# One input row loaded as 16 short rows and spread on the chip, with the query weights moved ahead in ScalarE's queue of loads

## The chip, the cores and the metric

The kernel runs on one NeuronCore of one Trainium2 chip. The metric is the device time of one launch in microseconds (us). Three runs of the kernel before gave a median of 193.31 us (193.21 to 193.57). One further execution was recorded by the hardware profiler. All durations and waits below come from that execution.

The core has five engines with a queue of instructions each: TensorE (PE; its loads of weights are shown as PEld), VectorE (DVE), ScalarE (ACT), GpSimd (POOL) and SyncE (SP). In this kernel SP and ACT also issue the DMAs, which 16 DMA engines carry out. The profile calls the DMA queue that SP fills q1 and the one that ACT fills q10.

## The reference

One token is decoded. With x of 512 values, the reference computes (cut to what matters):

```
xn = layernorm(x)
q  = xn @ wq                       # 32 heads of 128
s  = softmax(q k^T / sqrt(128)) v  # per head, the last 4096 of 32768 cached keys
s  = s @ wo                        # 4096 -> 512
x1 = xn + hs                       # hs = 0 here: a shift along a sequence of length 1
g  = silu(x1 + gelu(layernorm(x1) @ w3) @ w4)
out = x + s * g
```

All inputs are bfloat16. Keys and values of the window are 32 x 4096 x 128 values each, 33.6 MB each. The weights wq and wo have 4.2 MB each; w2, w3 and w4 have 3.3 MB together.

## The kernel before, in words

**Tiling.** The 32 heads are worked in 8 groups of G = 4. A group's keys are one tile `kv` of 128 partitions x 32768 bytes, 4.2 MB, and so are its values. The partitions hold 32 stretches of keys of each of 4 heads. K tiles come from a pool of three buffers, V tiles from a pool of two. The V pool (line 539) is opened in the place of the pool `wts`, which holds the weights wq, w2, w3, w4 and some small tiles of the head of the kernel, once these are done with.

**Scores.** Of each K tile, 64 or 80 of the 128 columns of keys go to VectorE, in four parts: `k_vector` multiplies by the query, spread over the partitions in `q_bc` (line 321), and adds up (line 323). The others are turned by TensorE (line 339), copied out by ScalarE (line 342) and multiplied by `q_pair` (line 350). Softmax and the values follow two steps behind (LAG = 2): `sm_exp` on ScalarE, `v_wide` on TensorE (line 427).

**Order.** The loop over steps (from line 533) is written out by hand for PE, DVE and ACT. Ahead of it, in the head of the kernel, a scheduler orders the instructions of each engine. SP's loads go through `load` (lines 75 and 76), which keeps them in the order of the program: w2, w3, w4 (two pieces), K of group 0 in two halves, K of group 1, K of group 2, V of group 0, K of group 3, and so on. A load into a buffer waits until its former reader is done. Eight completion semaphores of DMAs are given out in turn over SP's and ACT's loads together; a load that gets one which was used before waits for the landing of that earlier load first.

**The head.** ACT issues three loads (lines 79, 82 and 84):

- `x_bf`: x as 128 partitions of 4 values (128 rows of 8 bytes), for the layernorm;
- `x_row`: x as 4 rows of 128 values on partitions 0, 32, 64 and 96, after GpSimd has cleared the tile. `xn_row` (line 242) and the last addition (line 656) read it;
- `wq_sb`: the query weights, 128 rows of 32768 bytes.

Then line 183 turns `x_bf` into float32 `x_f`. `ln_stats` (lines 158 to 179) adds it up by TensorE and takes mean and variance. Lines 186 to 196 give `xq_bf`, the normed x in the order that wq wants. Lines 203 to 209 multiply it by wq (32 products, `qr_ps`). Lines 210 to 218 copy and spread the result into `q_bc`, and lines 219 to 226 make `q_pair`. Between them stand the multi-layer part (lines 228 to 280: a second layernorm, `a_ps` by line 252 with a gelu in line 255, w4 in line 270, `g_row` in line 280) and `make_masks` (lines 126 to 141), which makes small tables of ones and zeros from the identity for the end of the kernel.

**Places in memory.** The pools stand one behind the other in each partition: K, kt, prod, const, small, sm, and then wts (later the V pool). The first tile in `small` is an unused one of 192 bytes (line 71, `pad`). With it the K tiles start at bytes 16512, 49280 and 82048 of each partition, `wq_sb` at 151808, and the V tiles at 160000 and 192768.

**The end.** The last group's V comes in three pieces (64, 32 and 32 columns), and two loads of rows of wo follow it. After the last piece has landed come 32 products (line 461), a multiplication (line 471), 16 products with the rows of wo (line 155), lines 654 and 656, and the store.

Of the kernel before, what the change touches and what calls it, by code (L numbers as in the profile page):

```python
# [8 lines left out]
P = 128  # L9
BF16 = mybir.dt.bfloat16  # L10
FP32 = mybir.dt.float32
ACT = mybir.ActivationFunctionType
ALU = mybir.AluOpType
AX = mybir.AxisListType
# [12 lines left out]
def kernel(  # L27
# [14 lines left out]
    nc = tc.nc  # L42

    Bb, Sq, D = A_x.shape
    assert Bb == 1 and Sq == 1, "decode kernel: B == Sq == 1"
    _, H, Sk, Dh = A_k_cache.shape
    HD = A_wq.shape[1]
# [6 lines left out]
    KC = D // P  # L54
# [9 lines left out]
    small = ctx.enter_context(tc.tile_pool(name="small", bufs=1))  # L64
    ps_misc = ctx.enter_context(tc.tile_pool(name="ps_misc", bufs=1, space=PSUM))
# [7 lines left out]
    wts = wts_guard.__enter__()  # L73

    def load(dst, src):
        return tc.keep_in_program_order(nc.sync.dma_start(out=dst, in_=src))  # L76

    x_bf = small.tile([P, KC], BF16, name="x_bf")
    nc.scalar.dma_start(out=x_bf[:], in_=A_x.rearrange("a b (p c) -> p (a b c)", p=P))
    x_row = small.tile([P, P], BF16, name="x_row")  # L80
    nc.gpsimd.memset(x_row[:], 0.0)
    nc.scalar.dma_start(out=x_row[0:P:32, :], in_=A_x.rearrange("a b (j n) -> (a b j) n", j=KC))
    wq_sb = wts.tile([P, KC, HD], BF16, name="wq_sb")
    nc.scalar.dma_start(out=wq_sb[:].rearrange("p c n -> p (c n)"),
                        in_=A_wq.rearrange("(a b c) n -> b a (c n)", a=4, c=KC))
    w2_sb = wts.tile([P, KC, D], BF16, name="w2_sb")
    load(w2_sb[:], B_w2.rearrange("(p c) n -> p c n", p=P))
    w3_sb = wts.tile([P, KC, F], BF16, name="w3_sb")
# [14 lines left out]
    ident_bf = const.tile([P, P], BF16, name="ident_bf")  # L103
# [54 lines left out]
    def ln_stats(src_f, tag):  # L158
        ps = ps_misc.tile([P, KC], FP32, tag="misc", name="ln_ps")
        nc.tensor.matmul(ps[:], lhsT=ones_f[:], rhs=src_f, start=True, stop=True)  # L160
        tot = small.tile([P, 1], FP32, name=f"ln_tot_{tag}")
        nc.vector.reduce_sum(out=tot[:], in_=ps[:], axis=AX.X)
        negmean = small.tile([P, 1], FP32, name=f"ln_negmean_{tag}")
        nc.vector.tensor_scalar(out=negmean[:], in0=tot[:], scalar1=-1.0 / D,
                                scalar2=None, op0=ALU.mult)
        xc = small.tile([P, KC], FP32, name=f"ln_xc_{tag}")
        nc.vector.tensor_scalar(out=xc[:], in0=src_f, scalar1=negmean[:], scalar2=None,
                                op0=ALU.add)
        sq = small.tile([P, KC], FP32, name=f"ln_sq_{tag}")
        nc.vector.tensor_tensor(out=sq[:], in0=xc[:], in1=xc[:], op=ALU.mult)  # L170
        ps2 = ps_misc.tile([P, KC], FP32, tag="misc", name="ln_ps2")
        nc.tensor.matmul(ps2[:], lhsT=ones_f[:], rhs=sq[:], start=True, stop=True)
        vtot = small.tile([P, 1], FP32, name=f"ln_vtot_{tag}")
        nc.vector.reduce_sum(out=vtot[:], in_=ps2[:], axis=AX.X)
        rstd = small.tile([P, 1], FP32, name=f"ln_rstd_{tag}")
        nc.vector.tensor_scalar(out=rstd[:], in0=vtot[:], scalar1=1.0 / D,
                                scalar2=LN_EPS, op0=ALU.mult, op1=ALU.add)
        nc.gpsimd.tensor_tensor(out=rstd[:], in0=rstd[:], in1=neg_half[:, 0:1], op=ALU.pow)
        return xc, negmean, rstd


    x_f = small.tile([P, KC], FP32, name="x_f")
    nc.vector.tensor_copy(out=x_f[:], in_=x_bf[:])
    xc, negmean, rstd = ln_stats(x_f[:], "x")
    xn_f = small.tile([P, KC], FP32, name="xn_f")
    nc.vector.tensor_scalar(out=xn_f[:], in0=xc[:], scalar1=rstd[:], scalar2=None, op0=ALU.mult)
# [16 lines left out]
    for b in range(2):  # L203
        zeros(qr[b][:])
        for c in range(KC):
            wc = wq_sb[:, c, :].rearrange("p (g a d) -> p g a d", a=G, d=Dh)
            for a in range(G):
                nc.tensor.matmul(qr[b][32 * a:32 * a + 1], lhsT=xq_bf[:, c:c + 1], rhs=wc[:, 4 * b:4 * b + 4, a, :],  # L208
                                 start=False, stop=(c == KC - 1), skip_group_check=True)
    nc.scalar.copy(out=q_row[:, 0:4, 0, :], in_=qr[0][:])  # L210
    nc.vector.tensor_copy(out=q_row[:, 4:8, 0, :], in_=qr[1][:])  # L211
    for b in range(2):
        qb_ps = ps_tr.tile([P, 4, Dh], FP32, tag="pt", name="qb_ps")
        nc.tensor.matmul(qb_ps[:], lhsT=sel[:].rearrange("k b a -> k (b a)"), rhs=q_row[:, 4 * b:4 * b + 4, 0, :],
                         start=True, stop=True)
        nc.scalar.copy(out=q_bc[:, 4 * b:4 * b + 4, :], in_=qb_ps[:])
    for b in range(2):
# [5 lines left out]
        for t in range(2):  # L223
            rows = slice(64 * t, 64 * t + 64)
            nc.scalar.copy(out=q_pair[rows, 4 * b:4 * b + 4, :, G * t:G * t + G].rearrange("p g l a -> p g a l"),  # L225
                           in_=qt_ps[rows].bitcast(BF16).rearrange("p g (a m l) -> p g a m l", a=G, l=2)[:, :, :, 0, :])
# [4 lines left out]
    for j in range(KC):  # L231
        for c in range(KC):
            nc.tensor.matmul(hs_ps[:, j:j + 1], lhsT=w2_sb[:, c, j::4],
                             rhs=shifted_bf[:, c:c + 1], start=(c == 0), stop=(c == KC - 1))
# [30 lines left out]
    for i in range(11):  # L265
        n = P if i < 10 else 96
        terms.append((a_bf[0:n, i % 3, i // 3:i // 3 + 1], w4_sb[0:n, i, :]))
    for i, (col, w) in enumerate(terms):
        r = 32 * (i % 4)
        nc.tensor.matmul(hr_ps[r:r + 1].rearrange("r j n -> r (j n)"), lhsT=col, rhs=w, start=False,  # L270
                         stop=(i >= len(terms) - 4), skip_group_check=True)
# [25 lines left out]
                            op=ALU.max)  # L297
    par_t = const.tile([1 + G, PB, G], FP32, name="par_t")
    nc.vector.tensor_scalar(out=par_t[:],
                            in0=ident_f[0:1 + G, 1:1 + G].unsqueeze(1).to_broadcast([1 + G, PB, G]),  # L300
# [387 lines left out]
```

## Time and profile before

| what | us |
|---|---|
| median of 3 runs (range) | 193.31 (193.21 to 193.57) |
| the profiled execution, its own time | 193.37 |
| its span, first to last instruction | 191.2 |
| outside the span (193.37 - 191.2) | 2.2 |
| busy: DVE, PE, ACT, POOL | 150.9, 121.2, 89.5, 2.4 |
| share of q1 and q10 of the 16 DMA engines' span | 91.6%, 5.1% |
| bytes moved | 79.02 MB |

How to read it: the busy time of an engine is a sum over the whole span, and a high sum alone does not make it the bound. The span is also shown cut in 40 slices of 4.78 us, with a digit for the busy tenths of each engine and of the DMA engines. The windows view gives the same for any stretch of time, with the rate of the DMA engines. The chain of waits follows the end of the kernel back to what released each step. "Landing" is when the last of the DMA engines that took part reports that its share of a transfer is done. The trace also holds a record of every DMA packet: queue, start, duration and size. Here a packet is one row of a transfer.

### The profile page before, as it was taken

Reading aid. Unit: us, or ns where it says so; the run is one execution under the profiler, and the core shown is the slowest. Engines: PE = TensorE matmul, PEld = TensorE weight load, DVE = VectorE, ACT = ScalarE, POOL = GpSimd, SP = SyncE. Lnnn points to the kernel's source line nnn. Section 1 sums busy time; section 2 is a strip of 40 time slices with the busy share of each in tenths; the row PEclk is TensorE's granted clock in tenths of the full one; section 3 lists DMA queues with packets and bytes.
Section 4 is the critical chain, followed back from the end, with each engine's and each line's share of the span. In section 5 each row is a group of like instructions: output and inputs, shape, how many; then the busy total and the mean of one; then the engine's idle time right before and its main releaser. Section 6 shows DMA issues by size and latency. Waiting matters only on the chain.

```text
span 191.2 us, 2843 instructions
## 1 busy us (share of the span) xinstructions
PE 121.2 (63%) x1161; PEld 77.0 (40%) x1161; DVE 150.9 (79%) x175; ACT 89.5 (47%) x191; POOL 2.4 (1%) x11
## 2 busy tenths in 40 slices
PE   1554853989826368356945773681889289749772
PEld 0430222767615334243434432540764078513321
DVE  1560169979999999999999999999999997990111
ACT  2001270887795076527364654552575147743120
POOL 2110000000000000000000000000000000000000
PEclk9999696555665556955585579558555855996999
DMA  6999999999999999999999999999999998999990
GB/s 202 436 444 410 431 425 432 439 439 437 432 440 432 432 428 439 439 439 418 428 418 425 439 428 408 456 432 435 439 439 434 428 432 379 471 435 394 415 372 29
DMA packets 4572, 79.02 MB, mean 413 GB/s; under 512 B 624, under 2 KB 1232, under 8 KB 1488
## 3 DMA queue, kind: packets, MB, share of 16 engines
q1 hardware_dynamic: 4264, 74.65, 91.6%
q10 hardware_dynamic: 296, 4.20, 5.1%
q8 instruction: 9, 0.15, 0.3%
q14 instruction: 3, 0.02, 0.0%
HBM read 78.84 MB, written 0.00 MB: 412 GB/s over the span
## 4 chain that ended last, share of the span: by engine, by line
DVE 47%; DMA 42%; PE 6%; ACT 1%; issue 1%; SPq 1%; DVEq 0%; ACTq 0%
DMA kv<-in_A_k_cache_dram 31%; DVE S L323 28%; DVE prod L321 16%; DMA kv<-in_A_v_cache_dram 9%; PE pt L339 3%; DMA x_bf<-in_A_x_dram 2%; ACT kt L342 1%; PE ov L427 1%; PE sT L350 1%; DVE m L366 1%; SPq L76 1%; DVE S L364 1%; DVE mx L374 1%; PE oT L461 1%; PE ot_ps L444 0%
## 5 line engine op out<-in xcount | busy, mean ns | idle before, releaser
L323 DVE TENSOR_REDUCE S<-prod 128x20 f32<-128x2560 bf16 (+1 forms) x32 | 86.0, 2686 | 1.1
L342 ACT COPY kt<-pt 128x1024 bf16<-128x1024 bf16 x52 | 51.4, 1013 | 40.0 <-PE pt L339 38.1
L339 PE MATMUL pt<-ident_f,kv 128*128 128x128 f32 x208 | 49.2, 392 | 10.0 <-DMA kv<-in_A_k_cache_dram 10.0
L321 DVE TENSOR_TENSOR prod<-kv,q_bc 128x2560 bf16<-128x2560 bf16 (+1 forms) x32 | 45.4, 1417 | 3.6 <-ACT q_pair L225 1.8
L339 PEld LDWEIGHTS pt<-ident_f,kv 128*128 128x128 f32 x208 | 36.2, 205 | 13.9 <-DMA kv<-in_A_k_cache_dram 9.3
L350 PE MATMUL sT<-q_pair,kt 128*128 128x8 bf16 x416 | 19.6, 170 | 14.9 <-ACT kt L342 14.8
L350 PEld LDWEIGHTS <-kt 128*128 128x128 bf16 x416 | 16.9, 105 | 26.1 <-ACT kt L342 24.9
L427 PE MATMUL ov<-kv,pT 128*16 128x512 bf16 x248 | 23.2, 536 | 1.2 <-DMA kv<-in_A_v_cache_dram 1.2
L388 ACT ACTIVATE pT<-S,mb 128x128 bf16<-128x128 f32 x32 | 13.9, 572 | 0.3
L372 PE MATMUL mt_ps<-ident_f,m 128*1 128x128 f32 x8 | 2.9, 360 | 16.6 <-DVE rden L399 16.1
L433 ACT COPY ov_sb<-ov 128x512 f32<-128x512 f32 x8 | 4.7, 586 | 18.4 <-PE ov L427 18.4
L427 PEld LDWEIGHTS <-pT 128*16 128x16 bf16 x248 | 6.9, 112 | 14.3 <-issue 12.7
L359 ACT ACTIVATE own<-sT,par 128x48 f32<-128x48 f32 (+1 forms) x32 | 7.5, 356 | 3.7 <-PE sT L350 3.7
L444 PE MATMUL ot_ps<-ident_f,ov_sb 128*128 128x128 f32 x32 | 7.5, 379 | 2.2 <-ACT mb L384 1.7
L211 DVE CAST q_row<-qr_ps 128x512 bf16<-128x512 f32 x1 | 0.7, 692 | 10.0 <-PE qr_ps L208 10.0
L388 ACT ACTIVATION_READ_ACCUMULATOR pT<-S,mb 128x1 f32 x32 | 8.3, 258 | 0.0
L372 PEld LDWEIGHTS mt_ps<-ident_f,m 128*1 128x1 f32 x8 | 0.6, 80 | 17.1 <-DVE rden L399 16.4
L399 DVE RECIPROCAL rden<-den_ps 128x4 f32<-128x4 f32 x8 | 1.4, 175 | 6.7 <-PE den_ps L394 6.7
L381 PE MATMUL mb_ps<-md,par_t 5*128 5x4 f32 x16 | 3.9, 311 | 4.1 <-DVE md L376 4.1
L255 ACT ACTIVATE a_row<-a_ps 128x384 bf16<-128x384 f32 x1 | 0.5, 491 | 12.1 <-remote 12.1
L444 PEld LDWEIGHTS ot_ps<-ident_f,ov_sb 128*128 128x128 f32 x32 | 4.8, 188 | 3.2 <-ACT mb L384 2.1
L208 PE MATMUL qr_ps<-wq_sb,xq_bf 128*1 128x512 bf16 x32 | 3.5, 611 | 3.6 <-DMA wq_sb<-in_A_wq_dram 3.6
(122 smaller groups left out, 82.8 us busy)
## 6 DMA issues: line engine op xcount, KB each, us to landing
kv<-in_A_k_cache_dram SPq DMA_DIRECT2D x7, 4096.0 KB, 31.0
kv<-in_A_v_cache_dram SPq DMA_DIRECT2D x7, 4096.0 KB, 30.6
wq_sb<-in_A_wq_dram ACTq DMA_DIRECT2D x1, 4096.0 KB, 17.5
kv<-in_A_k_cache_dram SPq DMA_DIRECT2D x2, 2048.0 KB, 27.5
wo<-in_A_wo_dram SPq DMA_DIRECT2D x1, 2048.0 KB
kv<-in_A_v_cache_dram SPq DMA_DIRECT2D x1, 2048.0 KB
kv<-in_A_v_cache_dram SPq DMA_DIRECT2D x2, 1024.0 KB, 16.3
w_sb<-in_B_w_dram SPq DMA_DIRECT2D x1, 1376.0 KB, 10.3
```

The source lines that it names most:

```text
L208: nc.tensor.matmul(qr[b][32 * a:32 * a + 1], lhsT=xq_bf[:, c:c + 1], rhs=wc[:, 4 * b:4 * b + 4, a, :], start=False, stop=(c == KC - 1), sk ...
L321: nc.vector.tensor_tensor(out=prod[:, 0:m, :], in0=kn[:, rows, :], in1=q_bc[:, g:g + 1, :].to_broadcast([P, m, Dh]), op=ALU.mult)
L323: nc.vector.tensor_reduce(out=st[g]["S"][:, rows], in_=prod[:, 0:m, :], axis=AX.X, op=ALU.add)
L339: nc.tensor.transpose(pt[:, i, :], kn[:, c:c + 2, :].rearrange("p c d -> p (c d)").bitcast(FP32), ident_f[:])
L342: nc.scalar.copy(out=kts[b][:, 0:n, :], in_=pt[:, 0:n, :].bitcast(BF16))
L350: nc.tensor.matmul(st[g]["sT"][:, c:c + 2, :].rearrange("p c a -> p (c a)"), lhsT=kt[:, i, l::2], rhs=q_pair[:, g, l, :], start=(l == 0), ...
L359: nc.scalar.mul(s["own"][:, 0:m, a], s["sT"][:, 0:m, a], par[:, a:a + 1])
L381: nc.tensor.matmul(mb_ps[:], lhsT=par_t[:].rearrange("k b a -> k (b a)"), rhs=md[:], start=True, stop=True)
L388: nc.scalar.activation(out=s["pT"][:, :, a], in_=s["S"][:], func=ACT.Exp, scale=scale, bias=mb[:, a:a + 1], accum_out=s["sum"][:, a:a + 1])
L427: nc.tensor.matmul(ov[r:r + 4 * G], lhsT=s["pT"][:, c:c + 4, :].rearrange("p i a -> p (i a)"), rhs=v[:, c:c + 4, :], start=(i < 4), stop=( ...
L433: nc.scalar.copy(out=s["ov_sb"][:], in_=ov[:])
L444: nc.tensor.transpose(ot_ps[:, step * j:step * j + P], s["ov_sb"][:, j, :], ident_f[:])
```

## The change

```diff
-    x_bf = small.tile([P, KC], BF16, name="x_bf")
-    nc.scalar.dma_start(out=x_bf[:], in_=A_x.rearrange("a b (p c) -> p (a b c)", p=P))
+    XR, XC = 16, D // 16
+    x_in = small.tile([XR, XC], BF16, name="x_in")
+    nc.scalar.dma_start(out=x_in[:], in_=A_x.rearrange("a b (r n) -> (a b r) n", r=XR))
+    wq_sb = wts.tile([P, KC, HD], BF16, name="wq_sb")
+    nc.scalar.dma_start(out=wq_sb[:].rearrange("p c n -> p (c n)"),
+                        in_=A_wq.rearrange("(a b c) n -> b a (c n)", a=4, c=KC))
     x_row = small.tile([P, P], BF16, name="x_row")
     nc.gpsimd.memset(x_row[:], 0.0)
     nc.scalar.dma_start(out=x_row[0:P:32, :], in_=A_x.rearrange("a b (j n) -> (a b j) n", j=KC))
-    wq_sb = wts.tile([P, KC, HD], BF16, name="wq_sb")
-    nc.scalar.dma_start(out=wq_sb[:].rearrange("p c n -> p (c n)"),
-                        in_=A_wq.rearrange("(a b c) n -> b a (c n)", a=4, c=KC))
...
+    m8 = P // XR
+    x_up = wts.tile([XR, XR, m8], BF16, name="x_up")
+    nc.vector.tensor_copy(out=x_up[:], in_=ident_bf[0:XR, 0:XR].unsqueeze(2).to_broadcast([XR, XR, m8]))
+    x_own = wts.tile([P, m8], BF16, name="x_own")
+    nc.vector.tensor_reduce(out=x_own[:], in_=ident_bf[:].rearrange("d (i t) -> d t i", t=m8), axis=AX.X, op=ALU.max)
+    x_all = ps_misc.tile([P, m8, KC], FP32, tag="misc", name="x_all")
+    nc.tensor.matmul(x_all[:].rearrange("p t c -> p (t c)"), lhsT=x_up[:].rearrange("k r t -> k (r t)"), rhs=x_in[:],
+                     start=True, stop=True)
+    x_pick = wts.tile([P, m8, KC], FP32, name="x_pick")
+    nc.vector.tensor_tensor(out=x_pick[:], in0=x_all[:], in1=x_own[:].unsqueeze(2).to_broadcast([P, m8, KC]), op=ALU.mult)
     x_f = small.tile([P, KC], FP32, name="x_f")
-    nc.vector.tensor_copy(out=x_f[:], in_=x_bf[:])
+    nc.vector.tensor_reduce(out=x_f[:], in_=x_pick[:].rearrange("p t c -> p c t"), axis=AX.X, op=ALU.add)
```

x for the layernorm comes as 16 rows of 32 values. One product with `x_up` (ones where column d belongs to row d/8) repeats each row on 8 partitions, the table `x_own` keeps on each partition the four values that are its own, and a sum over the 8 places gives `x_f` as before. The load of wq is ACT's second, that of `x_row` its third.

What the built program shows of the change, beyond the diff:

- The tile `x_in` takes 64 bytes of each partition where `x_bf` took 32 (8, rounded up). All later tiles of `small`, `sm`, `wts` and the V pool start 32 bytes further on: `wq_sb` at 151840, V at 160032 and 192800. K stays where it was.
- The load of K of group 2 waits for the landing of wq, where it waited for `x_row`: it has been given the same completion semaphore.
- On DVE, most of `make_masks` stands between the steps of the first layernorm, where before it stood between those of the second; `xn_row` stands directly ahead of the copy `q_row` (before: ahead of `xq_bf`).
- On PE, the last of the 20 products of `a_ps` stands behind the 32 with wq. On ACT, a load of an activation table and the gelu of `a_row` follow the first copy into `q_row`, where before they stood ahead of it; there is one load of a table more.

## The prediction

> **What bounds the kernel now.** I read the windows view first, for the rate of the DMA engines:
>
> ```profile
> core 0: us, PE busy (x) PEld busy (x) DVE busy (x) ACT busy (x) POOL busy (x), PEclk, DMA share, GB/s
> 0.00:4.78 4.78, 0.61 (x1) 0.10 (x1) 0.52 (x6) 1.28 (x1) 1.24 (x9) 1.00 0.67 202
> 4.78:184.00 179.22, 117.17 (x1096) 75.15 (x1098) 149.43 (x165) 87.57 (x189) 1.11 (x2) 0.69 1.00 430
> 184.00:191.20 7.20, 3.43 (x70) 1.75 (x62) 0.98 (x4) 0.60 (x2) 0.00 (x0) 0.97 0.34 128
> ```
>
> From 4.78 to 184 us the 16 DMA engines are busy all the time (share 1.00) at 430 GB/s. The packet records agree: the first packet starts at 1.78 us, the last large one ends at 187.2 us, and a 32768-byte row takes 1213 ns (median) whatever it belongs to. 79.02 MB at 430 GB/s are 183.8 us; with 1.78 us ahead, some slow first packets, and what follows the last byte (187.2 to 191.2), that is the span. So the stream of bytes is the bound, if it never runs dry. The longest pieces of the chain of waits tell about that:
>
> ```profile
> 0.74 4.03 DMA x_bf<-in_A_x_dram
> 5.36 36.62 DMA kv<-in_A_k_cache_dram
> ...
> 130.42 23.05 DMA kv<-in_A_k_cache_dram
> 168.94 17.25 DMA kv<-in_A_v_cache_dram
> ```
>
> The chain puts x_bf at its head, since SP's fourth load of K waited for the semaphore of x_bf. It is not a cause: the K tile issued at 5.36 us landed 36.6 us later, and the records show its first row starting at 29.9 us. It stood in the queue for over 24 us. The load of the last group's V, issued from 168.9 us on, needs 17.25 us, of which its own 4.19 MB are 9.8 us at 430 GB/s: some 7 us of other work still stood ahead. At 130.4 us the same sum gives 13 us. So a delay of compute by less than about 7 us leaves the engines fed.
>
> Next, what waits in the head:
>
> ```profile
> 4.79 0.17 DVE L183 CAST x_f<-x_bf 128x4 f32<-128x4 bf16 x1 [3.45 <-DMA x_bf<-in_A_x_dram]
> ...
> 19.87 3.45 PE L208 MATMUL qr_ps<-wq_sb,xq_bf 128*1 128x512 bf16 x32 [3.61 <-DMA wq_sb<-in_A_wq_dram]
> ...
> 25.93 1.23 DVE L321 TENSOR_TENSOR prod<-kv,q_bc 128x2048 bf16<-128x2048 bf16 x1 [1.80 <-ACT q_pair L225]
> ...
> 42.08 1.49 DVE L321 TENSOR_TENSOR prod<-kv,q_bc 128x2560 bf16<-128x2560 bf16 x1 [1.32 <-DMA kv<-in_A_k_cache_dram]
> ```
>
> The x chain is done 3.61 us before wq lands (19.83). The first multiplication by K starts at 25.93; its K half landed at 25.83 and q_bc was written by 25.36, so here too a transfer is as late as the query. And before group 1, VectorE waits 1.32 us for K. The query therefore has slack twice, and both landings are set by the count of bytes ahead of them.
>
> **The change part by part.**
>
> *The load of x.* Removed: 128 rows of 8 bytes, 8 for each DMA engine, at 9 ns plus about 6 ns to the next packet: 8 x 15 = 0.12 us of each engine. Added: 16 rows of 64 bytes, one for each. The nearest rows are 9 ns (8 bytes) and 15 to 18 ns (256 bytes), some 0.02 us. Sum: -0.10 us on the stream, which is the path. x lands earlier too: the first x packets started between 2.17 and 2.9 us and the last at 4.24, with the landing at 4.76, so x_in should land between 3 and 4 us. That is off the path.
>
> *The start of the stream.* SP's first load (w2) is issued as before, at 0.73 us, and opens the stream at 1.78. The 256 packets of 4096 bytes (w2 and one later load) take 0.8 us per engine more than at their median of 159 ns, nearly all of it before 3.5 us: most first packets took 0.75 to 1.1 us, and started before any x packet. Packets behind the first x packet were slow in seven or so cases (256 to 756 ns). Bounds for what x_in changes here: 0 and -0.3 us (about 4 us of such excess over 16 engines). I take 0, as one x packet for each engine remains, and it was the first that was followed by the slow ones.
>
> *Spreading x.* Added on the x chain: a product (row of xq_ps: 0.16), x_pick on 128x32 (between 0.16 for 128x4 and 0.34 for 128x128), a sum in place of the cast (0.16 to 0.38 by the reductions L162 and L136), and two hand-overs between engines of 0.1 to 0.2. Together +0.6 to +1.2 us. x_up, x_own and perm are made while x is awaited. About ten mask operations of 0.18 to 0.38 us now stand between the steps of this chain, most in waits for TensorE, so I allow +1 us more; the second layernorm loses them. Cover: x lands some 1 us sooner, and PE's 3.61 us ahead of L208. Without cover the chain would be 2 us late, still inside it.
>
> *wq earlier.* Its issue moves from 2.29 to about 1.2 us (behind one issue of 0.40 instead of 0.40 and 1.09). It shares the engines with w2 to w4 and K, so it lands 0 to 1.1 us sooner, and K by as many bytes later until wq is in. The bytes ahead of the first K half (wq, w2 to w4 and that half: 9.6 MB) are the same, so its landing at 25.83 stays. Worth nothing on the path.
>
> *The query behind it on ACT.* Now the copy L210 (0.59), a load of a table (1.28, the row at 26.49), a_row (0.49), a copy (0.62) and two of q_bc (0.59 each) stand in one line. L210 started 1.79 us after wq; a_row has to wait for the product placed behind the 32 (3.45). So a_row ends about 4.2 us and q_bc 6.0 to 6.1 us behind wq, against 5.5 now: 0.5 us later, less what wq gains. The 1.32 us ahead of group 1 covers it.
>
> *x_row third.* It stands behind wq in ACT's queue and lands with it, between 0 and 2 us later. Behind its reader xn_row on DVE wait q_row's copy and all of k_vector, but that copy needs the 32 products, 3.5 us after wq. Hidden, and 1.32 us more if not.
>
> *K of group 2.* It waits for wq's semaphore: issue at about 19.9 instead of by 7.24 us (end of the stretch of four K issues). Queued ahead of it are 15.9 MB, 37 us at 430 GB/s; V of group 0 behind it on SP is not due before 30.98. 18 us of reserve.
>
> *32 bytes.* The tiles behind x_in move by 32 bytes. No transfer in this trace goes to such an offset: K starts 128 bytes past a multiple of 256, wq, w2 to w4 and V on one, x_row at 192 past. K rows and V rows both take 1213 ns, and x_row's 18 ns fit the line through 1024 and 4096 bytes (8.4 ns + 1.18 ns for each 32 bytes). Shifted are 2528 rows, 158 for each engine. Bounds: 0, or a second fixed part of 8.4 ns for each row, 1.3 us. I take 0, by K against V. [...]
>
> **Sum.** -0.10 + 0 + 0 + 0: the profiled execution of 193.37 becomes 193.27, and the median of 193.31, 0.06 below it, becomes 193.2.
>
> **The rivals.**
>
> *Shifted rows cost time (slower).* Each of the 158 rows per engine pays at the seam. It decides from 3 ns a row on (0.10 + 0.39 us over 158). With a second fixed part: 193.2 + 1.3 = 194.5. [...] For it: only multiples of 64 are seen to be free. Against: 64 and 128 cost nothing.
>
> *A better start (faster).* The slow early packets belong to x's 128 rows after all: 0.8 us off, 192.4. For it: slow packets behind x packets. Against: the first were slow before x.
>
> *A late query (slower).* ACT's line or xn_row makes the query more than 1.3 us late, all of K's releases follow, and the queue's reserve of 7 us at the last V is eaten. It needs over 8 us; the steps above give 0.5. Beyond that point, each us is one: 195 with 2.
>
> *It does nothing in the stream.* If x's small packets overlapped with waiting anyway: 193.3, inside the forecast.
>
> **How the numbers follow.** 0.2% (0.39 us) is about what a measurement of this kernel can tell from no change. Forecast, with the last rival: 0.58, 193.0 to 193.5. Shifted rows 0.28, more of it near 194.5 than at 205; late query 0.04; a better start 0.10. Hence faster 0.10, same 0.58, slower 0.32. The range leaves out the end of the faster case and what lies above a second fixed part: 192.7 to 194.8.
>
> **What would show it.** Right: the rate from 4.78 to 184 us is still 430 GB/s; PE still waits for wq ahead of its 32 products; K of group 2 is issued near 19 us, and the engines stay at a share of 1.00. Wrong: V's rows longer than 1213 ns with K's at 1213 (shifted rows); a share below 1.00 near 30 or 170 us (late query, or K of group 2); a first slice well over 202 GB/s (better start).

## The result, and the profile after

The kernel after took 193.93 us (median of 8 runs, 193.81 to 194.14) against 193.32 us (8 runs, 193.21 to 193.57) of the kernel before: ratio 1.0031, 95% interval 1.0022 to 1.0041, 0.6 us slower. The forecast was 193.2 us and no change. The time lies inside the range, but the direction was wrong, and the interval is clear of no change.

The windows view of the kernel after (PE, PEld, DVE, ACT and POOL busy, granted clock, share and rate of the DMA engines):

```profile
core 0: us, PE busy (x) PEld busy (x) DVE busy (x) ACT busy (x) POOL busy (x), PEclk, DMA share, GB/s
0.00:4.78 4.78, 1.36 (x5) 0.57 (x5) 2.40 (x16) 1.28 (x1) 1.23 (x9) 1.00 0.58 216
4.78:184.00 179.22, 115.50 (x1089) 73.79 (x1089) 148.51 (x158) 88.11 (x190) 1.10 (x2) 0.70 1.00 429
184.00:191.20 7.20, 3.58 (x70) 1.86 (x69) 0.98 (x4) 1.12 (x2) 0.00 (x0) 0.98 0.43 158
```

The engines are as full as before (share 1.00). The rate is 429 GB/s where it was 430, and 0.2% of 179 us is 0.4 us. More bytes are left for the last stretch: 158 GB/s there, against 128.

The longest pieces of the chain of waits, after (start, duration, what):

```profile
4.34 37.48 DMA kv<-in_A_k_cache_dram
...
130.65 23.08 DMA kv<-in_A_k_cache_dram
169.20 17.64 DMA kv<-in_A_v_cache_dram
```

The last group's V is issued 0.26 us later than before and needs 17.64 us instead of 17.25.

The head of the kernel after (start, duration, engine, line, what, and the idle time ahead with what ended it; lines of the head stand some 11 further down in this kernel):

```profile
4.13 0.20 DVE L194 TENSOR_REDUCE x_f<-x_pick 128x4 f32<-128x32 f32 x1
...
18.99 2.44 PE L219 MATMUL qr_ps<-wq_sb,xq_bf 128*1 128x512 bf16 x32 [2.29 <-DMA wq_sb<-in_A_wq_dram]
19.26 0.34 DVE L253 TENSOR_SCALAR xn_row<-x_row,ln_negmean_x,ln_rstd_x 128x128 f32<-128x128 bf16 x1 [6.54 <-DMA x_row<-in_A_x_dram]
...
25.90 1.23 DVE L332 TENSOR_TENSOR prod<-kv,q_bc 128x2048 bf16<-128x2048 bf16 x1 [2.57 <-DMA kv<-in_A_k_cache_dram]
```

Before, `x_f` was written by 4.96 us, and PE waited for wq until 19.87. So `x_f` is ready 0.6 us sooner, wq lands 0.9 us sooner, and the first multiplication by K starts where it did (25.93 before), now plainly waiting for K and not for the query. VectorE still waits ahead of group 1:

```profile
42.32 1.49 DVE L332 TENSOR_TENSOR prod<-kv,q_bc 128x2560 bf16<-128x2560 bf16 x1 [1.59 <-DMA kv<-in_A_k_cache_dram]
```

So the head is not what got slower. The 32 last products, which wait for the last piece of V, tell where the time came. Before:

```profile
186.24 0.96 PE L461 MATMUL oT<-pT,kv 128*128 128x4 bf16 x32 [0.18 <-DMA kv<-in_A_v_cache_dram]
```

After:

```profile
186.89 0.96 PE L472 MATMUL oT<-pT,kv 128*128 128x4 bf16 x32 [0.25 <-DMA kv<-in_A_v_cache_dram]
```

0.65 us later. The landings in the trace show it grow: K of group 1 lands 0.16 us sooner than before, V of group 0 is 0.04 us late at 61 us, V of group 4 is 0.27 us late at 144 us, and the last piece of V 0.65 us late at 186.8 us. Something took a little of many transfers.

The packet records name it. Before, 1213 ns is the shortest and by far the most frequent duration of a row of 32768 bytes (1471 of 1920). The table gives by tile, in the order of the queue, the share of its 128 rows that took exactly that. K1 is the K of group 1, V0 the V of group 0. The last two columns are the means of the 8192-byte rows (256 of the last V, 128 of wo) and of the 1024-byte rows, in ns:

```
                          K1   K2   V0   K3   V1   K4   V2   K5   V3   K6   V4   K7   V5   V6   8192   1024
before                   .23  .17  .88  .79  .92  .81  .90  .84  .89  .31  .94  .95  .95  .99  309.0  46.0
after                    .13  .20  .16  .18  .09  .15  .16  .21  .05  .30  .14  .45  .15  .00  313.9  47.9
after, unshifted         .09  .28  .90  .80  .88  .80  .91  .81  .86  .30  .91  .97  .98 1.00  309.0  46.0
before, all +32          .23  .27  .06  .20  .16  .20  .09  .19  .16  .25  .17  .41  .09  .00  314.2  47.9
before, V alone +32      .66  .30  .08  .23  .15  .17  .09  .22  .16  .31  .15  .40  .09  .66  313.9  46.0
K at 256, all else +32  1.00  .98  .88  .95  .88  .94  .92  .88  .67  .99  .96  .96  .66  .00  312.9  47.9
K at 256 alone           .98  .84  .92  .91  .82  .80  .98 1.00  .98  .99  .99  .98  .99 1.00  309.0  46.0
after, V and K at 256   1.00  .98  .98 1.00  .99 1.00  .98 1.00  .98  .99 1.00  .98 1.00 1.00  309.0  46.0
```

The first two lines are the result; the others are experiments below. After the change, most rows take longer (1493 of 1920): the most frequent duration is 1216 ns where it was 1213, and 1218 and 1224 ns come next among the longer ones. The line of before holds the warning that the prediction passed over: K1, K2 and K6 are already off 1213 there.

### The profile page after: what moved, and what is told of

The parts are those of the page before. It is cut to its first block, busy times and chain, and to the rows that moved or that the text cites. A ratio compares the mean times of both kernels' runs of the same rounds, so it can differ in the third digit from the quotient of the medians.

```text
span 191.8 us, 2851 instructions
## 1 busy us (share of the span) xinstructions
PE 120.4 (63%) x1162; PEld 76.2 (40%) x1162; DVE 151.9 (79%) x178; ACT 90.5 (47%) x192; POOL 2.3 (1%) x11
## 4 chain that ended last, share of the span: by engine, by line
DVE 47%; DMA 43%; PE 6%; ACT 1%; issue 1%; SPq 0%; DVEq 0%; ACTq 0%
DMA kv<-in_A_k_cache_dram 32%; DVE S L334 28%; DVE prod L332 15%; DMA kv<-in_A_v_cache_dram 9%; PE pt L350 3%; DMA w_sb<-in_B_w_dram 2%; ACT kt L353 1%; PE ov L438 1%; PE sT L361 1%; DVE m L377 1%; DVE S L375 1%; DVE mx L385 1%; PE oT L472 1%; PE ot_ps L455 0%; DVE md L387 0%
## 5 line engine op out<-in xcount | busy, mean ns | idle before, releaser
L350 PE MATMUL pt<-ident_f,kv 128*128 128x128 f32 x208 | 47.7, 382 | 10.0 <-DMA kv<-in_A_k_cache_dram 10.0
L350 PEld LDWEIGHTS pt<-ident_f,kv 128*128 128x128 f32 x208 | 35.1, 200 | 13.7 <-DMA kv<-in_A_k_cache_dram 11.2
L361 PE MATMUL sT<-q_pair,kt 128*128 128x8 bf16 x416 | 19.5, 170 | 14.9 <-ACT kt L353 14.7
L221 ACT CAST q_row<-qr_ps 128x512 bf16<-128x512 f32 x1 | 0.6, 585 | 15.8 <-PE qr_ps L219 15.8
L392 PEld LDWEIGHTS mb_ps<-md,par_t 5*128 5x128 f32 x16 | 3.6, 274 | 5.9 <-PE sT L361 4.6
```

The costliest lines, as they stand in the source:

```text
L350: nc.tensor.transpose(pt[:, i, :], kn[:, c:c + 2, :].rearrange("p c d -> p (c d)").bitcast(FP32), ident_f[:])
L361: nc.tensor.matmul(st[g]["sT"][:, c:c + 2, :].rearrange("p c a -> p (c a)"), lhsT=kt[:, i, l::2], rhs=q_pair[:, g, l, :], start=(l == 0), ...
L392: nc.tensor.matmul(mb_ps[:], lhsT=par_t[:].rearrange("k b a -> k (b a)"), rhs=md[:], start=True, stop=True)
```

## The experiments

Theory A: the 32 bytes by which `x_in` pushes the weights, V and the rows of wo off a multiple of 256 lengthen the rows of the transfers, and the rest of the change is a small gain (a place that is not a multiple of 256 is called off 256 below, and "32 past" means 32 bytes past a multiple). Theory H, the rival: the new order of loads in the head sets how the 16 engines run against each other from then on, and the place is harmless. Each kernel was timed in 5 rounds against the kernel before.

**The change without the shift** (e1_after_unshifted).

```diff
 # the kernel after
-    small.tile([P, 96], BF16, name="pad")
+    small.tile([P, 80], BF16, name="pad")
```

> The kernel after, with the unused first tile of the pool small 32 bytes shorter (160 instead of 192), so that wq, w2 to w4, V and the rows of wo stand at the places of the kernel before. Theory A (the shifted places make each row of a transfer longer; the mean of V's 32768-byte rows was 1221 ns after against 1217 before, the 8192-byte rows 313.9 against 309.0): the rows go back to 1213 and 309 ns (medians) and the time to 193.2 us, the 193.32 of before less 0.1 for x's fewer packets. Theory H (the head's other order of loads sets how the 16 engines run against each other, and the place does not matter): the rows stay at 1216 and 313 and the time stays near 193.9.

Measured: 192.99 us against 193.39 of before beside it, ratio 0.9983 (0.9974 to 0.9991). The rows are back at 1213 and 309 ns (third line of the table), and the last products start at 186.14:

```profile
186.14 0.96 PE L472 MATMUL oT<-pT,kv 128*128 128x4 bf16 x32 [0.16 <-DMA kv<-in_A_v_cache_dram]
```

Theory A holds, H does not. Taking 32 unused bytes out turns the change from 0.31% slower into 0.17% faster, a difference of 0.48% or 0.93 us. The change itself is worth 0.33 us, three times what was forecast for it.

The packets' durations account for most of the difference. Added up over all packets but those of w2 at the start, they are 0.70 us per engine more in the profiled execution of the kernel after than in the unshifted one (183.3 against 182.6), and its last large packet ends 0.74 us later (187.8 against 187.1).

**The shift alone** (e2_before_plus32).

```diff
 # the kernel before
-    small.tile([P, 96], BF16, name="pad")
+    small.tile([P, 112], BF16, name="pad")
```

> The kernel before, with the unused first tile of small 32 bytes longer (224 instead of 192): the shift of the change and nothing else of it. Theory A: V's rows at 1216 to 1224 ns and the 8192-byte rows at 314, the time 0.6 to 0.7 us over before, 193.9 to 194.0. Theory H: 193.3, rows at 1213 and 309.

Measured: 194.16 us, ratio 1.0046 (1.0034 to 1.0058), 0.89 us. The rows look like those of the kernel after, and the last products start later still (the profiled execution was the slowest of five, 194.48 us):

```profile
187.19 0.96 PE L461 MATMUL oT<-pT,kv 128*128 128x4 bf16 x32 [0.25 <-DMA kv<-in_A_v_cache_dram]
```

The shift suffices without anything else of the change, and costs a little more than the 0.6 to 0.7 us that theory A gave. The same sum of durations is 0.78 us over that of before, with the last large packet 0.89 us later.

**Other offsets** (e3_before_plus64 and e4_before_plus128): the same edit, with 128 and 160 in place of 112.

> The kernel before with the same tile 64 bytes longer, so V starts 64 bytes past a multiple of 256. Theory A with a seam at multiples of 64 only: 193.3, rows at 1213. Theory A with a seam at multiples of 256, or any offset: 193.9 or more. Theory H: 193.3.

> The kernel before with the same tile 128 bytes longer, so V starts 128 bytes past a multiple of 256, as K does. Theory A with a seam at 64 or 128: 193.3. With a seam at 256: V's rows longer than 1213, 193.6 to 194. Theory H: 193.3.

Measured: 193.96 us, ratio 1.0036 (1.0024 to 1.0048), and 194.05 us, ratio 1.0042 (1.0030 to 1.0054). The 8192-byte rows took 313.6 and 313.3 ns on average. 64 and 128 bytes past cost about as much as 32 (sum of durations 0.69 and 0.67 us over before). Of the offsets tried (32, 64 and 128 past) none is free. K, which all these kernels hold 128 past, then should not be free either.

**V alone shifted** (f2_v_alone_plus32).

```diff
 # the kernel before, in V's pool, behind wo_rows and ahead of V
+            v_pool.tile([P, 16], BF16, tag="vpad", bufs=1, name="vpad")
```

> The kernel before with V's two buffers alone 32 bytes further on (an unused tile of 32 bytes ahead of them in V's own pool); the weights, the rows of wo and all small tiles stay where they were. If it is the rows of transfers that pay, V carries nearly all of it (35 of the 42 MB shifted): 193.9 to 194.1, the 8192-byte rows at 313. If it is the engines' own reads and writes of the small tiles (S, pT, q_bc and others moved too), 193.4 and 309.

Measured: 193.88 us, ratio 1.0027 (1.0016 to 1.0037). The 8192-byte rows take 313.9 ns, the 1024-byte rows, which are not V's, 46.0 as before. V's place accounts for more than half of the shift's cost. The rest, some 0.4 us, is left for the weights and the rows of wo; no run moved these alone, and the intervals of the two runs overlap slightly.

**The small tiles alone shifted** (g3_small_alone_plus32).

```diff
 # the kernel before
-    small.tile([P, 96], BF16, name="pad")
+    small.tile([P, 112], BF16, name="pad")
...
     y_sum = small.tile([P, D], FP32, name="y_sum")
+    small.tile([P, 112], BF16, name="pad2")
```

> The kernel before with the small tiles alone 32 bytes further on, and 224 unused bytes behind them, so that the weights and V move by 256 in all and stay on multiples of 256. If only the transfers' rows pay: 193.3 to 193.4, as before, rows at 1213 and 309. If the engines' small tiles pay: 193.6 or more.

Measured: 193.34 us, ratio 1.0003 (0.9994 to 1.0011): no difference. The tiles of the pool `small`, which the compute engines read and write, may stand 32 bytes further on; that leaves the transfers' rows. The tiles of `sm` moved by 256 here and were not tried alone; with V alone shifted they had not moved, and the cost was there.

**The 16 rows alone, and the order alone** (f3_rows_alone, f4_order_alone): the kernel after with ACT's loads back in the order x, x_row, wq, and the kernel before with wq ahead of x_row; the places are those of before in both.

```diff
 # f3: the kernel after
-    small.tile([P, 96], BF16, name="pad")
+    small.tile([P, 80], BF16, name="pad")
 # and wq_sb with its load moved back behind the load of x_row
 # f4: the kernel before, wq_sb with its load moved ahead of x_row
```

> The 16 rows of x and their spreading alone: ACT's loads in the order of before (x, x_row, wq), places as in before. The version with all of the change but the shift took 192.99, 0.4 under the 193.39 beside it. If that comes from the 128 small packets (w2's rows at the start of the stream were 0.40 us per engine shorter in sum, and the packets themselves are 0.06 us of busy time): 193.0. If it comes from wq's earlier place: 193.4.

> The order alone: x_bf as in before, 128 rows, but wq second and x_row third; places as in before. If the gain of the unshifted version is that of the small packets: 193.4, as before (K of group 2 issued near 19 us for nothing). If it is the order's: 193.0. If waiting for x_row or for wq's semaphore costs: over 193.6.

Measured: 193.14 us, ratio 0.9990 (0.9981 to 0.9999) for the rows, and 193.27 us, 0.9997 (0.9988 to 1.0006) for the order. The order by itself is no difference that can be told, in either direction, though K of group 2 waits for wq in it. The 16 rows are a gain. In the packet records its place is the start of the stream: w2's 128 rows of 4096 bytes took 1.83 to 2.22 us per engine in the nine profiled kernels that load x as 128 rows, and 1.51 to 1.73 us in the four with 16 rows. The means are 1.97 and 1.63, so 0.34 us. With the packets themselves, 0.06, that is near the 0.33 us of the first experiment; the 0.19 us (0.02 to 0.37) of the rows alone is compatible with it, and so is a small share for the order. It is not shown that all of it reaches the end: in the profiled executions of the unshifted version and of the rows alone, the last large packet ends only 0.14 and 0.21 us sooner than in that of before.

**K on a multiple of 256 too** (f1_k_and_v_at_256), the version that follows from the above:

```diff
 # the kernel after
+    ctx.enter_context(tc.tile_pool(name="kpad", bufs=1)).tile([P, 64], BF16, name="kpad")
     k_pool = ctx.enter_context(tc.tile_pool(name="k", bufs=K_BUFS))
...
-    small.tile([P, 96], BF16, name="pad")
+    small.tile([P, 16], BF16, name="pad")
```

> The kernel after with V and the weights back on multiples of 256 bytes and, new, K too: 128 unused bytes ahead of the K pool, the unused tile of small 32 bytes. So no large transfer starts off a multiple of 256. If every row off 256 costs (theory A for K as well): K's first two tiles, 1217 to 1226 ns a row on average before, go to 1213, worth at most 2 x 8 rows x 8 ns = 0.13 us per engine, as the later K rows are at 1213 already: 192.9 against the 192.99 of the version with V alone put back. If K's 128 bytes are free: 193.0, and the rows of the first two K tiles stay at 1217.

Measured: 192.65 us against 193.35, ratio 0.9963 (0.9949 to 0.9977). It beats both kernels. All but a few rows take 1213 ns (last line of the table), and its windows view has 431 GB/s:

```profile
4.78:184.00 179.22, 111.68 (x1098) 69.90 (x1099) 148.44 (x159) 88.24 (x191) 1.10 (x2) 0.73 1.00 431
184.00:191.20 7.20, 2.82 (x62) 1.64 (x60) 0.98 (x4) 0.48 (x1) 0.00 (x0) 0.85 0.28 105
```

The gain over the unshifted version, 0.34 us, is more than the 0.13 us that the rows of K1 and K2 could give. The records bear it out: the sum of durations is 0.33 us per engine under that of the unshifted version, 0.19 of it in the 32768-byte rows, and the last large packet ends 0.35 us sooner. K6 gains as well (table). But the sum of the single gains (0.17% and the 0.08% below) stays under 0.37%, though inside the intervals; why K's move gains more in the new kernel than alone is open.

**K alone, and K with the shift** (g2_k_at_256_alone: the first edit above in the kernel before, the unused tile at 32 values; g1_k_at_256_v_plus32: the same with 48, so that all but K stands 32 past).

> The kernel before with K alone moved onto a multiple of 256 (128 unused bytes ahead of the K pool, the unused tile of small 128 bytes shorter); nothing else of the change. The kernel with the change, V put back and K moved too took 192.65 against 192.99 without K's move. If K's place gives that by itself: 193.0 to 193.1 against 193.35, with all 32768-byte rows at 1213. If the gain needs the new head: 193.3.

> The kernel before with the shift of the change (weights, V and rows of wo 32 bytes past a multiple of 256) but with K moved onto a multiple of 256. It asks why K's rows, which the change did not move, went from 1213 to 1216 ns. If a row pays only for its own start: K's rows at 1213 throughout, V's at 1216 to 1224, and the time 0.2 to 0.3 us under the 194.16 of the shift alone, 193.9. If rows that start off 256 also hold up the rows of the other tile beside them: K's rows stay at 1216 and the time near 194.1.

Measured: K alone 193.20 us, ratio 0.9992 (0.9983 to 1.0000), half of what was expected and at the edge of what can be told; the sum of durations is 0.05 us under before. K with the shift 193.69 us, ratio 1.0019 (1.0010 to 1.0028), below the shift without it (1.0046), as the first case had it, and by more. But neither case had all the rows right. K's rows were at 1213 in 88% to 100% of cases, as the first case had it. V's rows, 32 bytes past, took 1213 ns here in 66% to 96% of cases from V0 to V5, and in none at V6. V6 stands behind rows of wo that are off 256 too, and the last V behind V6; V0 to V5 stand behind K or wo rows that are on one. The line of before says the same with the parts exchanged: K1 and K2 (behind other K), and K6 (behind rows of wo in a K buffer) are off, while K3, K4 and K5, each behind a V tile on 256, are mostly at 1213. V alone shifted is the direct test: K was not moved there, and the share of K3, K4 and K5's rows at 1213 fell from between 79% and 84% to between 17% and 23%. So in these runs the rows of a tile off a multiple of 256 mostly took longer when the transfer ahead of them in the queue was off one too (17% to 23% of K3, K4 and K5 at 1213); behind one on a multiple most kept 1213 (79% to 84% of the same before, 66% to 96% of V0 to V5 here). The shares are not sharp. K1, with the same place and the same transfer ahead of it, had 23% before, 66% with V alone shifted and 45% with the small tiles alone shifted, and with every large tile on a multiple (K alone) V1 and K4 had 82% and 80%. Why the transfer ahead matters stays open; no run here shows what happens inside a transfer.

## Why the prediction was wrong, point by point

- **The bound** held: the stream of bytes, never dry (share 1.00 from 4.78 to 184 us), sets the end. Every shift that made the kernel slower lengthened the rows, by 0.28 to 0.78 us in sum.
- **32 bytes** is the step that failed. It was taken at 0 "by K against V", with 1.3 us as the other end; the runs give 0.93 us (after against unshifted) and 0.89 us (the shift alone). The reason failed in its reading of the trace. The median over all rows was 1213 ns, so K at 128 past looked free. Taken tile by tile, the same trace has medians of 1217 and 1218 ns in K1 and K2 and 1215 in K6. K's other rows were at 1213 because V, on 256, stood ahead of them: with V alone shifted, most of them left it. A median over a mixture hid the one condition that the change was about to spread to all. The rival "shifted rows cost time" was the right one. Its 194.5 had the cost in the right place, the rows, and the price too high; the 205 named beside it is shown by no run, as the slowest of the shifted kernels took 194.16. "64 and 128 cost nothing" was false (ratios 1.0036 and 1.0042). The sign given for it came half: V's rows grew, but K's, which were to stay at 1213, grew with them (K3 from 79% at 1213 to 18%), as V ahead of them was now off 256.
- **The load of x and the start of the stream**, -0.10 and 0 (bounds 0 and -0.3): the runs give 0.33 us together. The rival "a better start" had this mechanism too, at 0.8 us. That the first slow packets came before any x packet was a poor reason to expect nothing: of the 0.34 us, 0.24 lie in the first 16 packets of w2 (means 0.70 and 0.46 us per engine), which in all but one of the 13 executions had started before any x packet. How the load of x lengthens packets ahead of its own is not shown.
- **The load that waits for x_bf** is the second half of group 0's K (issued at 4.78 us), not SP's fourth load of K, which waited for `x_row` (issued at 6.70). Nothing in the sum hangs on it.
- **Spreading x, wq earlier, the query on ACT, x_row, K of group 2**: costed at nothing, and the order alone is nothing (0.9997). By the trace: the two hand-overs estimated at 0.1 to 0.2 us took 0.04 (the product to `x_pick`) and 0.15 (`x_f` to the first product of `ln_stats`), PE waits 2.29 us for wq, x_row lands 0.3 us behind it, the query is written by 23.94 us, well ahead of its K (25.81), although the table load stands in its line; K of group 2 is issued by 19.5 us with the engines full. A wait that was not listed: the products of `a_ps` wait 1.61 us for w3, which lands at 13.73 us instead of 11.45, as wq now shares the engines sooner (13.97 with the order alone). It is hidden as well.
- **The sum**: -0.33 us for the head (the unshifted version) and +0.89 for the shift, measured by itself, give +0.56, against the measured +0.6.

## What to carry to other kernels

When transfers are the bound, look at what a change of a small tile does to the addresses of the large ones behind it: here 32 bytes cost more than the change gained (0.93 us against 0.33), and the version with every large tile on a multiple of 256 bytes was the fastest measured (192.65 us). Read the duration of rows tile by tile, in the order of the queue, before calling a price zero; a median over all of them is a statement about the most frequent neighbour (1213 ns over all, where K1 and K2 had 1217 and 1218). And look at the rows of the other transfers around a load of many tiny rows at the start of the stream: here its own time was 0.07 us per engine, and the rows of w2 took 0.34 us longer.

## What the runs showed of the hardware that was not expected

A 32768-byte row into a tile on a multiple of 256 bytes mostly took 1213 ns: 80% to 100% of the rows of each such tile in the table. With K 128 past and the other tiles 32 past (the kernel after), 22% of them did and 76% took 1214 to 1224 ns; the 8192-byte rows took 313.9 ns on average against 309.0, the 1024-byte rows 47.9 against 46.0. V, weights and rows of wo at 64 and 128 past cost much the same: 8192-byte rows of 313.6 and 313.3 ns, and a sum of durations 0.69 and 0.67 us over before, where 32 past had 0.78. A row seems to need an off-256 transfer ahead of it in the queue as well: V at 32 past behind K on 256 stayed at 1213 in 88% of V0's rows. And with 128 rows of 8 bytes in place of 16 of 64, 0.07 us of busy time per engine against 0.01, the 4096-byte rows at the start of the stream took 0.34 us per engine longer.
